# Another order for the opening of a feed-forward part: where the first block of M, the sums and the weight conversions are issued

## The chip, the core and the metric

The kernel runs on one core of a Trainium2 chip. The metric is the device time of one launch in microseconds (us). The profile names the engines as follows: PE is the matrix engine (PEld its weight load), DVE the vector engine, ACT the engine for activation functions, POOL the general engine, SP the engine that issues the loads. Each engine works through its own instructions in program order and waits at an instruction until what it reads is there and what it writes to is free.

## The reference

Three stages follow each other. Attention over 4 x 512 local tokens (a band of +-32 positions and 32 global tokens) and 4 x 32 global tokens gives x, 2176 rows of 512. A soft mixture of experts gathers x into 32 slots, runs an expert of two matrices on every slot, and hands the results back to the tokens by a second softmax. The last stage is a feed-forward part without a bias:

```python
    slot_out = slot_out.reshape(n_slots, D)
    c = np.exp(logits - logits.max(1, keepdims=True))
    c /= c.sum(1, keepdims=True) + 1e-09
    x = (c @ slot_out).astype(np.float32)
    h = x @ w_in
    g = h - np.tanh(h)
    return (g @ w_out).astype(np.float32)
```

All inputs and outputs are float32.

## The kernel before

The kernel never forms x of the last stage: h = c @ (slot_out @ w_in), and M = slot_out @ w_in has only 32 rows and 2048 columns. M and c are held in parts of rounded float32 (a high part and a remainder, 128 partitions in all), so that one rounded matmul of M against c gives h. g = h - tanh(h) is formed for small h as a polynomial, g_scaled = h (u - 2.5) u with u = h squared, and a flag computed at the end decides whether an exact second pass is needed.

The output is made of 17 tiles of 128 tokens. The feed-forward part runs in steps; a step is one chunk `fc` of 128 rows of w_out for a group of six (or five) tiles. One step: two heads (`g_head`, a matmul of 128x384 into one of two PSUM banks `h`, given out by `hbank()`), for each half of the tiles the square on ACT (`g_square`, line 1168), two operations on DVE (`g_tail0`, line 1174; `g_tail1`, line 1178, the last reader of the `h` bank), the rounded high part on ACT (`g_hi`, line 1185), the low part on POOL (`g_lo`, line 1189), and then per tile three matmuls (`ff`, lines 1202 to 1204): high x high, high x low, low x high of g and w_out, added up over the chunks in PSUM bank `a0` to `a5` of the tile. `gs_r` holds three sets of g, so heads run up to three steps ahead.

w_out comes as 64-bit words. `conv_head(c)` (ACT, line 535) and the four entries of `f32_tail` (an empty one, then DVE lines 539, 544, 549) turn chunk c into float32, `conv_ops(c)[4]` rounds it to `whi` (ACT, line 1062) and `[5]` makes `wlo` (POOL, line 1063). So `c1[1]`, `c1[2]`, `c1[3]` are DVE steps of chunk 1, `c1[4]` is ACT, `c1[5]` POOL.

The opening stands between the experts and the steps; it is written out by hand, line by line, and each engine gets its instructions in that order. The last expert matmuls (line 1036) leave the slot sums in `sop`, PSUM bank 5. They are scaled and copied to `sos` (line 1276), transposed and added up by four matmuls with `istk` (line 1279) and copied to `soT` (line 1280). Then M is made in blocks of 128, 384, 512, 512 and 512 columns: `m_rows(i, j)` (PE, line 1111, bank j), `m_rows_out(i)` (ACT, line 1120), `m_parts(i, j)` (PE, line 1125), `m_hi(i)` (ACT, line 1129) and `m_lo(i)` (DVE, line 1133). Blocks 0 to 2 fall in the opening; block 0 is all that the heads of step 0 need, block 1 serves the heads of steps 1 to 3. `keep_warm` (line 647) is a matmul whose result nobody reads. After the opening a loop over the steps follows; its first pass is step 1, `ff(1, ..)`.

Of the kernel before, what the change touches and what calls it, by code (L numbers as in the profile page):

```python
# [11 lines left out]
AF = mybir.ActivationFunctionType  # L12
ALU = mybir.AluOpType
# [49 lines left out]
def band_attention_soft_moe_tanhshrink_kernel(  # L63
# [15 lines left out]
    V, S, G, T, DMA = nc.vector, nc.scalar, nc.gpsimd, nc.tensor, nc.sync  # L79
# [454 lines left out]
    def f32_head(a, raw):  # L534
        S.activation(out=a.bitcast(F32), in_=raw[:, :, 1].bitcast(F32), func=AF.Abs, scale=2.0 ** -112)
# [110 lines left out]
    def keep_warm(bank, n):  # L646
        T.matmul(bank[:, 0:n], lhsT=ident, rhs=win[0][:, 0:n], skip_group_check=True)

    with tc.manual_schedule():
# [43 lines left out]
        for it in range(NG + 1):  # L693
# [33 lines left out]
            if gs is not None:  # L727
                c = global_probs(gs)
# [51 lines left out]
        f, rr = mrun[:, 10:11], mrun[:, 11:12]  # L780
# [31 lines left out]
        def diagonal(t, outer, n, step):  # L812
            return bass.AP(t.tensor, t.offset, [t.ap[0], (outer, n), (step + 4, 4), (1, 4)])
# [18 lines left out]
        whi, wlo, raw_o, val_t = {}, {}, {}, {}  # L832
# [66 lines left out]
        for g in range(2):  # L899
            V.tensor_copy(  # L900
                out=diagonal(siT[g][:, :, 16 * g:], 128, 4, 32),
                in_=sit[:, 0:128].rearrange("p (k g e s) -> p g k e s", k=4, g=2, e=4)[:, g],
# [12 lines left out]
        def bank(j):  # L915
            return psa.tile([128, 512], F32, tag=f"a{j}", name=f"a{j}")
# [4 lines left out]
        sop = bank(5)  # L921
# [126 lines left out]
        def conv_head(c):  # L1048
            if c < 16:
                f32_head(cv[0][:, c % 2], raw_o[c][0])  # L1050

        def conv_ops(c):
            if c >= 16:
                return [lambda: None] * 6
            raw, own = raw_o[c]
            r = slot(True)[0].rearrange("p (a f) -> p a f", a=2)
            whi[c], wlo[c] = r[:, 0, :].bitcast(F32R), r[:, 1, :].bitcast(F32R)
            w = cv[0][:, c % 2]
            wf = w.bitcast(F32)

            return f32_tail(w, raw, own) + [
                lambda: S.copy(out=whi[c], in_=wf),  # L1062
                lambda: G.tensor_tensor(out=wlo[c], in0=wf, in1=r[:, 0, :], op=ALU.subtract),  # L1063
            ]

        for u, (m, e) in enumerate(UNITS):
# [15 lines left out]
            k = CTURN.index(u) if u in CTURN else None  # L1082
            if k is not None:
                combine_turn(4 * k, 4 if k < 4 else 1)
            k = CPREP.index(u) if u in CPREP else None
# [21 lines left out]
        def m_rows(i, j):  # L1107
            lo, n = BLOCKS[i]
            pp = (hbank() if j is None else bank(j))[:, 0:n]
            for dc in range(4):  # L1110
                T.matmul(
                    pp[32 * dc:32 * dc + 32, :], lhsT=soT[:, dc, :], rhs=win[4 * (lo // 512) + dc][:, lo % 512:lo % 512 + n],
                    skip_group_check=True, tile_position=(0, 32 * dc),
                )
            mp_t[i] = pp

        def m_rows_out(i):
            n = BLOCKS[i][1]
            ms_t[i] = wk.tile([128, 512], F32, tag="sm", name="ms")[:, 0:n]
            S.copy(out=ms_t[i], in_=mp_t[i])  # L1120

        def m_parts(i, j):
            lo, n = BLOCKS[i]
            mp = (hbank() if j is None else bank(j))[:, 0:n]
            T.matmul(mp, lhsT=irep_m, rhs=ms_t[i])
            mp_t[i] = mp

        def m_hi(i):
            S.copy(out=mst(*BLOCKS[i]), in_=mp_t[i])

        def m_lo(i):
            lo, n = BLOCKS[i]
            V.tensor_tensor(
                out=mst(lo, n)[64:128], in0=mp_t[i][64:128, :], in1=mst(lo, n, F32)[64:128], op=ALU.subtract
            )
# [6 lines left out]
        gs_r = [[slot(True)[0][:, 0:768].bitcast(F32R) for _ in range(2)] for _ in range(3)]  # L1142
        n_u = 0
        steps = [(t0, nt, fc, fc == a, fc == b - 1) for t0, nt, a, b in PHASES for fc in range(a, b)]
        u_t, acc_t, part_t, room = {}, {}, {}, []
# [9 lines left out]
        def g_head(i, part):  # L1155
            nonlocal n_u
            t0, nt, fc = steps[i][:3]
            c = cols(i, part)
            n = c.stop - c.start
            h = hbank()[:, 0:n]  # L1160
            T.matmul(h, lhsT=mst(128 * fc, 128), rhs=cst(128 * t0 + c.start, n))  # L1161
            u, g = (r[:, n_u % 2, 0:n] for r in (u_r, g_r))
            n_u += 1
            u_t[i, part] = h, u, g

        def g_square(i, part):
            h, u, _ = u_t[i, part]
            S.activation(out=u, in_=h, func=AF.Square)  # L1168
# [3 lines left out]
        def g_tail0(i, part):  # L1172
            h, u, _ = u_t[i, part]
            V.scalar_tensor_tensor(out=h, in0=u, scalar=-2.5, in1=h, op0=ALU.add, op1=ALU.mult)  # L1174

        def g_tail1(i, part):
            h, u, g = u_t[i, part]
            V.tensor_tensor(out=g, in0=u, in1=h, op=ALU.mult)  # L1178
# [4 lines left out]
        def g_hi(i, part):  # L1183
            g, ghi, _ = g_parts(i, part)
            S.copy(out=ghi, in_=g)  # L1185

        def g_lo(i, part):
            g, ghi, glo = g_parts(i, part)
            G.tensor_tensor(out=glo, in0=g, in1=ghi.bitcast(F32), op=ALU.subtract)  # L1189
# [5 lines left out]
        def ff(i, tiles):  # L1195
            t0, nt, fc, first, last = steps[i]
            ghi, glo = gs_r[i % 3]
            for j in tiles:
                if first:
                    acc_t[j] = bank(tile_order(t0, nt).index(j))  # L1200
                c = slice(128 * j, 128 * j + 128)
                T.matmul(acc_t[j], lhsT=ghi[:, c], rhs=whi[fc], start=first, stop=False)  # L1202
                T.matmul(acc_t[j], lhsT=ghi[:, c], rhs=wlo[fc], start=False, stop=False)  # L1203
                T.matmul(acc_t[j], lhsT=glo[:, c], rhs=whi[fc], start=False, stop=last)  # L1204

        def keep_part(t0, j, scale):
            if not room:
                room.extend(two_rows())
            part_t[t0 + j] = room.pop(0)
            S.activation(out=part_t[t0 + j], in_=acc_t[j], func=AF.Copy, scale=scale)  # L1210
# [52 lines left out]
                V.tensor_reduce(out=am1, in_=amp, op=ALU.max, axis=AX.X)  # L1263
                V.tensor_scalar(out=flag, in0=am1, scalar1=THRESH, scalar2=None, op0=ALU.is_le)

        keep_warm(bank(0), 512)
        conv_head(0)
        c0 = conv_ops(0)
        c0[0]()
        c0[1]()  # L1270
        c0[2]()
        c0[3]()
        c0[4]()
        c0[5]()
        sos = wk.tile([128, 512], F32, tag="pt", name="sos")
        S.activation(out=sos, in_=sop, func=AF.Copy, scale=rr)
        sot = hbank()[:, 0:128]
        for dc in range(4):
            T.matmul(sot[:, 32 * dc:32 * dc + 32], lhsT=sos[:, 128 * dc:128 * dc + 128], rhs=istk, skip_group_check=True)
        V.tensor_copy(out=soT.rearrange("p k s -> p (k s)"), in_=sot)  # L1280
        conv_head(1)
        m_rows(0, 3)
        m_rows(1, 2)
        m_rows_out(0)
        c1 = conv_ops(1)
        c1[0]()
        m_rows(2, 3)
        c1[1]()
        m_parts(0, 0)
        c1[2]()  # L1290
        m_rows_out(1)
        m_parts(1, 2)
        c1[3]()
        m_hi(0)
        m_rows_out(2)
        m_lo(0)
        m_hi(1)
        g_head(0, 0)
        m_lo(1)
        c2 = conv_ops(2)  # L1300
        g_head(0, 1)
        g_square(0, 0)
        g_tail0(0, 0)
        g_tail1(0, 0)
        m_parts(2, 2)
        c1[4]()
        g_square(0, 1)
        g_head(1, 0)
        conv_head(2)
        g_tail0(0, 1)  # L1310
        c2[0]()
        keep_warm(bank(1), 256)
        g_hi(0, 0)
        g_square(1, 0)
        c1[5]()
        g_tail1(0, 1)
        g_tail0(1, 0)
        m_hi(2)
        g_hi(0, 1)
        g_head(1, 1)  # L1320
        c2[1]()
        g_lo(0, 0)
        ff(0, [0])
        g_lo(0, 1)
        ff(0, [1])
        g_square(1, 1)
        g_tail1(1, 0)
        g_tail0(1, 1)
        m_lo(2)
        g_hi(1, 0)  # L1330
        g_head(2, 0)
        g_square(2, 0)
        g_tail1(1, 1)
        g_lo(1, 0)
        ff(0, [4])
        g_tail0(2, 0)
        c2[2]()
        ff(0, [5])
        g_head(2, 1)
        g_hi(1, 1)  # L1340
        ff(0, [3])
        g_tail1(2, 0)
        ff(0, [2])
        g_square(2, 1)
        g_hi(2, 0)
        g_lo(1, 1)
        conv_head(3)
        g_tail0(2, 1)
        g_lo(2, 0)
        g_head(3, 0)  # L1350
        c2[3]()
        g_tail1(2, 1)
        g_square(3, 0)
        c2[4]()
        c2[5]()
        g_hi(2, 1)
        g_lo(2, 1)
        es_x.close()
# [1 line left out]
        for i, (t0, nt, fc, first, last) in enumerate(steps):  # L1360
# [4 lines left out]
            c = JOBS.get(i)  # L1365
# [3 lines left out]
            for part, tiles in enumerate((order[:half], order[half:])):  # L1369
# [43 lines left out]
                if part == 0:  # L1413
                    c = JOBS.get(i + 1)
# [32 lines left out]
    with tc.If(small < 1):  # L1447
        for t0, nt in [(0, 4), (4, 2), (6, 4), (10, 2), (12, 3), (15, 2)]:
            steps[:] = [(t0, nt, fc, fc == 0, fc == 15) for fc in range(16)]
            for i in range(18):  # L1450
                if i < 16:
# [3 lines left out]
                    u, g = (r[:, i % 2, 0:n] for r in (u_r, g_r))  # L1455
                    g_any(h, u, g, n)
                    ghi, glo = (x[:, 0:n] for x in gs_r[i % 3])
# [74 lines left out]
```

## Time and profile before

| | us |
|---|---|
| median of 3 runs | 403.67 (403.52 to 405.17) |
| profiled execution, its own time | 406.07 |
| its span, first to last instruction | 404.2 |
| PE busy | 380.3 (94%) |
| DVE busy | 275.7 (68%) |
| ACT busy | 218.2 (54%) |
| POOL busy | 208.3 (52%) |

The views show one profiled execution, with times from the start of its span. Ends of matmuls on PE are modelled. In a row with "xN" several instructions that follow each other on an engine are drawn together. "idle before" is the time for which the engine had nothing to do before the row, and the releaser is what ended it; a wait for several things is put down to the last one. An engine's share of the span is a mean over stages with different limits, so the stages are read one by one. The attention and the experts take the first 176 us, the opening lies between 175.8 and 184.7 us, and the steps of the feed-forward part fill the rest.

### The profile page before, as it was taken

The page shows a single profiled execution, that of the slowest core. Times are in us where ns is not written, and L with a number is a line of the kernel's source. Part 1 is how long each engine was busy: PE and PEld are TensorE (multiplying, and loading weights), DVE is VectorE, ACT ScalarE, POOL GpSimd, SP SyncE. Part 2 cuts the span into 40 slices and gives each one's busy share as a digit, 9 for nine tenths or more (in the row PEclk, how much of TensorE's full clock was granted, in tenths as well). Part 3 has the DMA queues.
Part 4 walks back from the last instruction along what each step waited for, and adds up shares of the span by engine and source line. Part 5 has one row for each costly group of instructions (what it writes and reads, how often), then busy time and mean ns, then how long its engine had stood idle before and what let it go on. Part 6 is the DMA issues. An engine that isn't in the chain of part 4 may idle for free.

```text
span 404.2 us, 10208 instructions
## 1 busy us (share of the span) xinstructions
PE 380.3 (94%) x3767; PEld 281.2 (70%) x3767; DVE 275.7 (68%) x832; ACT 218.2 (54%) x543; POOL 208.3 (52%) x275
## 2 busy tenths in 40 slices
PE   7979989989889899999999999999989999999994
PEld 3768778777677433336877786886868888888873
DVE  3577788776565546349998886697879997556541
ACT  2667877875566202248655645565575555445330
POOL 2567686666553010017866344455575667447441
PEclk9899999999999999999999999999999999999998
DMA  7799999999868899998203101003000003003004
GB/s 180 203 397 315 352 329 293 367 313 309 309 199 280 269 358 418 418 421 319 90 7 99 52 1 54 0 11 113 34 2 2 0 26 131 0 2 125 32 2 138
DMA packets 33978, 70.43 MB, mean 174 GB/s; under 512 B 3840, under 2 KB 10752, under 8 KB 33920
## 3 DMA queue, kind: packets, MB, share of 16 engines
q1 hardware_dynamic: 33776, 69.56, 50.8%
q8 instruction: 32, 0.52, 0.5%
q14 instruction: 26, 0.21, 0.2%
q10 hardware_dynamic: 144, 0.13, 0.1%
HBM read 65.22 MB, written 4.46 MB: 172 GB/s over the span
## 4 chain that ended last, share of the span: by engine, by line
PE 68%; DMA 9%; POOL 8%; issue 6%; DVE 5%; ACT 2%; SPq 0%; DVEq 0%; POOLq 0%; ACTq 0%
PE a L1204 13%; PE a L1203 13%; PE a L1202 13%; PE sc L248 8%; DMA slot<-in_w_dram 8%; PE X L281 4%; PE h L1161 4%; PE ptp L269 3%; POOL q L210 3%; PE gsc L434 3%; POOL slot L1189 2%; POOL v L210 2%; PE xgp L479 1%; DVE slot L1178 1%; POOL k L210 1%
## 5 line engine op out<-in xcount | busy, mean ns | idle before, releaser
L1189 POOL TENSOR_TENSOR slot<-slot 128x384 fp32r<-128x384 f32 x96 | 98.6, 1031 | 83.5 <-ACT slot L1185 81.6
L1202 PE MATMUL a<-slot 128*128 128x512 f32 x272 | 107.2, 394 | 1.3 <-ACT v_w L1210 0.7
L1204 PE MATMUL a<-slot 128*128 128x512 f32 x272 | 107.7, 396 | 0.0
L1203 PE MATMUL a<-slot 128*128 128x512 f32 x272 | 107.3, 394 | 0.0
L1174 DVE SCALAR_TENSOR_TENSOR h<-slot,h 128x384 f32<-128x384 f32 x96 | 51.5, 537 | 39.0 <-ACT slot L1168 38.7
L1185 ACT CAST slot<-slot 128x384 fp32r<-128x384 f32 x96 | 47.6, 496 | 49.0 <-DVE slot L1178 48.6
L1168 ACT ACTIVATE slot<-h 128x384 f32<-128x384 f32 x96 | 45.3, 473 | 34.9 <-PE h L1161 34.4
L1202 PEld LDWEIGHTS a<-slot 128*128 128x128 f32 x272 | 51.1, 188 | 13.8 <-ACT v_w L1210 1.4
L1204 PEld LDWEIGHTS a<-slot 128*128 128x128 f32 x272 | 51.0, 188 | 11.6
L1203 PEld LDWEIGHTS a<-slot 128*128 128x128 f32 x272 | 51.1, 188 | 9.2 <-POOL slot L1063 1.0
L1178 DVE TENSOR_TENSOR slot<-slot,h 128x384 f32<-128x384 f32 x96 | 50.9, 530 | 7.7 <-DVE h L1174 0.5
L258 ACT ACTIVATE sm<-sm,mb 128x128 f32<-128x128 f32 x128 | 41.2, 397 | 19.0 <-DVE mb L254 18.8
L248 PE MATMUL sc<-k,q 128*64 128x128 f32 x512 | 39.7, 297 | 4.8 <-POOL q L210 2.5
L248 PEld LDWEIGHTS sc<-k,q 128*64 128x64 f32 x512 | 33.8, 208 | 10.4 <-issue 5.1
L210 POOL TENSOR_SCALAR v<-v 32x1300 f32<-32x1300 f32 (+5 forms) x40 | 33.3, 833 | 12.7 <-PE xgp L479 8.6
L1063 POOL TENSOR_TENSOR slot<-k_w,slot 128x512 fp32r<-128x512 f32 x16 | 20.7, 1297 | 33.3 <-ACT slot L1062 33.3
L210 POOL TENSOR_SCALAR q<-q 64x256 f32<-64x256 f32 x62 | 28.1, 453 | 18.0 <-PE sc L248 7.9
L1161 PE MATMUL h<-slot 128*128 128x384 f32 x96 | 32.5, 341 | 0.8 <-DVE slot L1178 0.6
L254 DVE CUSTOM_DVE_ANT_0 sm<-sc,mask 128x128 f32<-128x128 f32 x128 | 30.1, 285 | 4.3 <-PE sc L248 3.8
L1161 PEld LDWEIGHTS h<-slot 128*128 128x128 f32 x96 | 17.9, 187 | 12.0 <-DVE slot L1178 5.9
L281 PE MATMUL X<-v,pt 128*32 128x65 f32 x1024 | 22.7, 223 | 2.4 <-issue 2.0
L281 PEld LDWEIGHTS X<-v,pt 128*32 128x32 f32 x1024 | 16.6, 109 | 7.3 <-issue 6.0
(244 smaller groups left out, 529.2 us busy)
## 6 DMA issues: line engine op xcount, KB each, us to landing
slot<-in_w_dram SPq DMA_DIRECT2D x54, 512.0 KB, 8.7
slot<-in_w_out_dram SPq DMA_DIRECT2D x9, 512.0 KB, 4.5
slot<-in_w_in_dram SPq DMA_DIRECT2D x16, 256.0 KB, 7.1
k<-in_k_dram SPq DMA_DIRECT2D x7, 576.0 KB, 8.0
q<-in_q_dram SPq DMA_DIRECT2D x15, 256.0 KB, 6.5
out_dram<-o SPq DMA_DIRECT2D x15, 256.0 KB, 2.4
slot<-in_w_in_dram SPq DMA_DIRECT2D x7, 512.0 KB, 9.8
v<-in_v_dram SPq DMA_DIRECT2D x8, 390.0 KB, 5.8
```

The lines of the kernel that those rows point to most:

```text
L210: G.tensor_scalar(out=o, in0=i, scalar1=0.0, scalar2=1.0, op0=ALU.add, op1=ALU.mult)
L248: T.matmul(sc[64 * i:64 * i + 64, a, :], lhsT=q_b[2][:, 256 * i + jj:256 * i + 256:4], rhs=k[:, i, :, WINDOWS[t][jj][0]], skip_group_check ...
L281: T.matmul(X[32 * jj:32 * jj + 32, h, :], lhsT=pt[:, 128 * jj + 32 * h:128 * jj + 32 * h + 32], rhs=v[:, WINDOWS[t][jj][0], 65 * h:65 * h ...
L1161: T.matmul(h, lhsT=mst(128 * fc, 128), rhs=cst(128 * t0 + c.start, n))
L1168: S.activation(out=u, in_=h, func=AF.Square)
L1174: V.scalar_tensor_tensor(out=h, in0=u, scalar=-2.5, in1=h, op0=ALU.add, op1=ALU.mult)
L1178: V.tensor_tensor(out=g, in0=u, in1=h, op=ALU.mult)
L1185: S.copy(out=ghi, in_=g)
L1189: G.tensor_tensor(out=glo, in0=g, in1=ghi.bitcast(F32), op=ALU.subtract)
L1202: T.matmul(acc_t[j], lhsT=ghi[:, c], rhs=whi[fc], start=first, stop=False)
L1203: T.matmul(acc_t[j], lhsT=ghi[:, c], rhs=wlo[fc], start=False, stop=False)
L1204: T.matmul(acc_t[j], lhsT=glo[:, c], rhs=whi[fc], start=False, stop=last)
```

## The change

The opening is issued in another order, and nothing is computed differently. The copy of the sums is cut into two halves of 256 columns, one on ACT and one on DVE. The warm-up matmul ahead of them has 256 columns in place of 512. Head and DVE steps of chunks 1 and 2 of w_out are issued earlier, partly ahead of the sums' copies. `m_rows` and `m_parts` use other banks, and `m_parts(0)` goes ahead of `m_rows(2)`. The first three tiles of step 0 are multiplied in two goes (`ff_first`): first the two terms with the high part of g, later the term with the low part; the remaining three tiles follow one by one between the heads of steps 1 and 2. Before, step 0 was multiplied tile by tile, in the order 0, 1, 4, 5, 3, 2, with both heads of step 1 ahead of it and the heads of step 2 between the tiles.

```diff
--- before.py
+++ after.py
@@ -1203,6 +1203,15 @@
                 T.matmul(acc_t[j], lhsT=ghi[:, c], rhs=wlo[fc], start=False, stop=False)
                 T.matmul(acc_t[j], lhsT=glo[:, c], rhs=whi[fc], start=False, stop=last)
 
+        def ff_first(terms, tiles):
+            ghi, glo = gs_r[0]
+            for j in tiles:
+                if terms.start == 0:
+                    acc_t[j] = bank(j)
+                c = slice(128 * j, 128 * j + 128)
+                for k, (g, w) in list(enumerate(((ghi, whi[0]), (ghi, wlo[0]), (glo, whi[0]))))[terms]:
+                    T.matmul(acc_t[j], lhsT=g[:, c], rhs=w, start=k == 0, stop=False)
+
         def keep_part(t0, j, scale):
             if not room:
                 room.extend(two_rows())
@@ -1263,96 +1272,90 @@
                 V.tensor_reduce(out=am1, in_=amp, op=ALU.max, axis=AX.X)
                 V.tensor_scalar(out=flag, in0=am1, scalar1=THRESH, scalar2=None, op0=ALU.is_le)
 
-        keep_warm(bank(0), 512)
         conv_head(0)
         c0 = conv_ops(0)
-        c0[0]()
-        c0[1]()
-        c0[2]()
-        c0[3]()
-        c0[4]()
-        c0[5]()
+        for f in c0:
+            f()
+        conv_head(1)
+        c1 = conv_ops(1)
+        c1[1]()
+        keep_warm(bank(0), 256)
         sos = wk.tile([128, 512], F32, tag="pt", name="sos")
-        S.activation(out=sos, in_=sop, func=AF.Copy, scale=rr)
+        S.activation(out=sos[:, 0:256], in_=sop[:, 0:256], func=AF.Copy, scale=rr)
+        V.tensor_scalar(out=sos[:, 256:512], in0=sop[:, 256:512], scalar1=rr, scalar2=None, op0=ALU.mult)
         sot = hbank()[:, 0:128]
         for dc in range(4):
             T.matmul(sot[:, 32 * dc:32 * dc + 32], lhsT=sos[:, 128 * dc:128 * dc + 128], rhs=istk, skip_group_check=True)
+        c1[2]()
+        conv_head(2)
         V.tensor_copy(out=soT.rearrange("p k s -> p (k s)"), in_=sot)
-        conv_head(1)
         m_rows(0, 3)
         m_rows(1, 2)
         m_rows_out(0)
-        c1 = conv_ops(1)
-        c1[0]()
-        m_rows(2, 3)
-        c1[1]()
-        m_parts(0, 0)
-        c1[2]()
+        c1[3]()
+        c2 = conv_ops(2)
+        c2[1]()
+        c1[4]()
+        c1[5]()
+        m_parts(0, 5)
+        m_rows(2, 1)
         m_rows_out(1)
-        m_parts(1, 2)
-        c1[3]()
+        c2[2]()
         m_hi(0)
+        m_lo(0)
+        g_head(0, 0)
+        g_head(0, 1)
         m_rows_out(2)
-        m_lo(0)
-        m_hi(1)
-        g_head(0, 0)
-        m_lo(1)
-        c2 = conv_ops(2)
-        g_head(0, 1)
+        m_parts(1, 4)
         g_square(0, 0)
+        c2[3]()
         g_tail0(0, 0)
         g_tail1(0, 0)
-        m_parts(2, 2)
-        c1[4]()
         g_square(0, 1)
+        m_parts(2, 5)
+        m_hi(1)
+        keep_warm(bank(0), 256)
+        g_hi(0, 0)
+        g_tail0(0, 1)
+        g_lo(0, 0)
+        g_tail1(0, 1)
+        m_hi(2)
+        ff_first(slice(0, 2), range(3))
+        g_hi(0, 1)
+        m_lo(1)
+        g_lo(0, 1)
         g_head(1, 0)
-        conv_head(2)
-        g_tail0(0, 1)
-        c2[0]()
-        keep_warm(bank(1), 256)
-        g_hi(0, 0)
         g_square(1, 0)
-        c1[5]()
-        g_tail1(0, 1)
+        ff_first(slice(2, 3), range(3))
+        m_lo(2)
+        c2[4]()
+        c2[5]()
         g_tail0(1, 0)
-        m_hi(2)
-        g_hi(0, 1)
+        ff(0, [3])
         g_head(1, 1)
-        c2[1]()
-        g_lo(0, 0)
-        ff(0, [0])
-        g_lo(0, 1)
-        ff(0, [1])
         g_square(1, 1)
         g_tail1(1, 0)
+        g_hi(1, 0)
+        g_lo(1, 0)
+        ff(0, [4])
         g_tail0(1, 1)
-        m_lo(2)
-        g_hi(1, 0)
         g_head(2, 0)
         g_square(2, 0)
         g_tail1(1, 1)
-        g_lo(1, 0)
-        ff(0, [4])
+        g_hi(1, 1)
+        g_lo(1, 1)
+        ff(0, [5])
         g_tail0(2, 0)
-        c2[2]()
-        ff(0, [5])
         g_head(2, 1)
-        g_hi(1, 1)
-        ff(0, [3])
+        g_square(2, 1)
         g_tail1(2, 0)
-        ff(0, [2])
-        g_square(2, 1)
         g_hi(2, 0)
-        g_lo(1, 1)
+        g_lo(2, 0)
         conv_head(3)
         g_tail0(2, 1)
-        g_lo(2, 0)
         g_head(3, 0)
-        c2[3]()
         g_tail1(2, 1)
         g_square(3, 0)
-        c2[4]()
-        c2[5]()
         g_hi(2, 1)
         g_lo(2, 1)
         es_x.close()
```

## Rows read from the trace of the kernel before

**Rows 1.** Stage table: busy time of each engine, granted clock, DMA share, GB/s.

```profile
core 0: us, PE busy (x) PEld busy (x) DVE busy (x) ACT busy (x) POOL busy (x), PEclk, DMA share, GB/s
175.80:184.70 8.90, 7.72 (x47) 3.55 (x47) 5.23 (x11) 6.22 (x14) 1.98 (x2) 1.00 1.03 420
189.50:396.50 207.00, 205.15 (x903) 162.76 (x902) 155.39 (x269) 112.52 (x245) 120.30 (x114) 1.00 0.12 41
```

**Rows 2.** Timeline of PE, 160 to 190: start, duration, instructions, [idle before, releaser].

```profile
176.69 0.97 PE L1279 MATMUL h<-istk,sos 128*128 128x32 f32 x8
178.05 1.93 PE L1111 MATMUL a<-win,mask 128*32 128x128 f32 x24 [0.38 <-DVE mask L1280]
179.92 1.14 PE L1125 MATMUL a<-ms,mask 128*128 128x128 f32 x4
181.09 0.62 PE L1161 MATMUL h<-slot 128*128 128x384 f32 x2
...
184.47 0.45 PE L1161 MATMUL h<-slot 128*128 128x384 f32 x1 [0.18 <-DVE slot L1178]
184.75 0.40 PE L1202 MATMUL a<-slot 128*128 128x512 f32 x1
...
189.53 0.40 PE L1202 MATMUL a<-slot 128*128 128x512 f32 x1
```

**Rows 3.** Timeline of ACT, 160 to 190, the steps of the chain.

```profile
175.85 0.69 ACT L1276 ACTIVATE sos<-a,mrun 128x512 f32<-128x512 f32 x1 [1.72 <-PE a L1036]
176.44 0.66 ACT L535 ACTIVATE k_w<-v_w 128x512 f32<-128x512 f32 x1
178.60 0.27 ACT L1120 COPY ms<-a 128x128 f32<-128x128 f32 x1 [1.51 <-PE a L1111]
179.25 0.48 ACT L1120 COPY ms<-a 128x384 f32<-128x384 f32 x1 [0.38 <-PE a L1111]
180.44 0.27 ACT L1129 CAST slot<-a 128x128 fp32r<-128x128 f32 x1 [0.72 <-PE a L1125]
...
183.41 0.52 ACT L1185 CAST slot<-slot 128x384 fp32r<-128x384 f32 x1
...
186.60 0.49 ACT L1168 ACTIVATE slot<-h 128x384 f32<-128x384 f32 x1 [0.22 <-PE h L1161]
```

**Rows 4.** Timeline of DVE, 160 to 190, the steps of the chain.

```profile
177.71 0.29 DVE L1280 COPY mask<-h 128x128 f32<-128x128 f32 x1 [4.23 <-PE h L1279]
177.91 0.42 DVE L539 TENSOR_SCALAR k_w<-k_w 128x512 int32<-128x512 int32 x1
178.37 0.69 DVE L544 SCALAR_TENSOR_TENSOR k_w<-v_w,k_w 128x512 int32<-128x512 int32 x1
...
180.74 0.29 DVE L1133 TENSOR_TENSOR slot<-a,slot 64x128 fp32r<-64x128 f32 x1 [0.96 <-ACT slot L1129]
...
182.21 0.56 DVE L1174 SCALAR_TENSOR_TENSOR h<-slot,h 128x384 f32<-128x384 f32 x1
182.80 0.55 DVE L1178 TENSOR_TENSOR slot<-slot,h 128x384 f32<-128x384 f32 x1
183.27 0.56 DVE L1174 SCALAR_TENSOR_TENSOR h<-slot,h 128x384 f32<-128x384 f32 x1
```

**Rows 5.** Timeline of SP: the issue of chunk 1 and a later issue.

```profile
166.04 0.33 SPq L104 DMA_DIRECT2D v_w<-in_w_out_dram  x1
...
176.07 0.33 SPq L104 DMA_DIRECT2D slot<-in_w_in_dram  x1
```

**Rows 6.** DMA issues, 165.5 to 166.5: count, size, us from issue to landing.

```profile
v_w<-in_w_out_dram SPq DMA_DIRECT2D x1, 512.0 KB, 10.0
```

**Rows 7.** Timeline of POOL, 160 to 190.

```profile
184.00 1.01 POOL L1189 TENSOR_TENSOR slot<-slot 128x384 fp32r<-128x384 f32 x1
```

**Rows 8.** Stage table of the start, columns as in the first group.

```profile
6.00:7.90 1.90, 0.01 (x1) 0.00 (x1) 0.85 (x9) 1.68 (x2) 0.00 (x0) 1.00 0.80 233
8.90:12.10 3.20, 3.20 (x27) 2.20 (x26) 1.72 (x11) 1.39 (x4) 1.30 (x4) 0.50 0.32 98
```

## The prediction

> **What bounds the kernel now.** I read the stage table first. From 189.5 us to 396.5 us TensorE is busy 205.15 of 207.00 us at a granted clock of 1.00 [rows 1]: in the feed-forward part PE is the bound, and nothing in that part changes. So whatever the opening gains or loses arrives at the end one for one, as the shift of one event: the first matmul of step 1, `ff(1, ..)`, at 189.53 [rows 2]. It is the first work after the edited stretch that both kernels issue in the same order. The opening, 175.80 to 184.70, is the other kind of stage: PE has 7.72 us of work in 8.90 us and no engine is full [rows 1], so there a chain of dependent steps sets the time. Read in order, it is: sum copy `sos` 175.85, its transposes 176.69, `soT` copied by 178.00, rows of M from 178.05, `m_parts` 179.92, first head 181.09, `g_hi(0,0)` 183.41, first `ff` 184.75 [rows 2 to 4]. From 184.75 to 189.53 PE issues the 18 matmuls of step 0 and three heads: 4.78 us, which 0.233 us a matmul and 0.2 us a head account for.
>
> **Part 1, the sums.** Before, ACT copies all 512 columns in 0.69 us and the transposes follow 0.15 us after its end [rows 2, 3]. After, ACT takes 256 columns and DVE 256. No row has that size; the ends are 0.27 (128 columns, ACT) or 0.29 (DVE) and 0.69 us (512) [rows 3, 4], I take 0.42 for both, near the middle as the column count is. Alone this would save about 0.3 us. But two other steps are moved ahead of it. `conv_head(1)` now stands before the ACT half, `c1[1]` before the DVE half. Both engines work in program order, and `conv_head(1)` reads chunk 1 of w_out, whose load SP issued at 166.04 [rows 5]. Loads of that stretch land 10.0 us after issue [rows 6], and SP's eighth issue after it comes at 176.07 [rows 5], which is 10.0 us on as well: the queue moves at the pace of the landings. So the data are there at about 176.05, after the last matmul that the sums need (the old copy could start at 175.85). Before, `conv_head(1)` came at 176.44, behind the copy [rows 3], and hid the load completely. Now the added wait holds the sums behind it:
> - ACT: `conv_head(1)` 176.07 to 176.73 (0.66), its half 0.10 us before that ends (as at 176.44 against 176.54 [rows 3]), 176.63 to 177.05.
> - DVE: `c1[1]` 176.78 (0.42), the DVE half 0.46 us later (177.91 to 178.37 [rows 4]), 177.24 to 177.66.
> - PE: the second half of the transposes starts 0.15 us later at 177.81 and takes half of 0.97 [rows 2]: 178.30. `c1[2]`, now ahead of the `soT` copy on DVE, takes 0.69 [rows 4] and ends at 178.35, so it is hidden, just. `soT` 178.35 to 178.64, against 178.00: **0.64 us later**.
>
> `conv_head(2)`, also moved up, reads a load issued one place later, there at about 177.3; ACT is free from 177.05 until the first `m_rows_out`, so it costs nothing. No DMA is issued in the moved steps, and SP's order is the same.
>
> The Trainium skill, DMA: Bandwidth & Descriptors, section Anatomy of one DMA, fits the time of a DMA as about 2.0 us plus its bytes over 436 GB/s; for 512 KB this is an estimate of 3.2 us, so chunk 1 would be there by 169.3 and the moved head would be free. It is a fit for another issuing path; the 10.0 us of the trace speaks against it here, and by it the time would be that of the first rival below.
>
> **Part 2, from `soT` to the first head.** Before: 178.00 to 181.09, 3.09 us. `m_rows(2, 3)` stood in front of `m_parts(0)` on PE, and had to wait for bank 3; so `m_parts(0)` began at 179.92 although its input was copied by 178.87 [rows 2, 3]. After, `m_parts(0, 5)` is in front. Then ACT is next: `m_rows_out(0)` 0.55 us after the rows start (178.05 to 178.60), at 179.24 to 179.51; `c1[4]` (512 columns on ACT, like the 0.66 row) must wait for `c1[3]` on DVE (178.56 to 179.25) and runs 179.5 to 180.1; then `m_rows_out(1)` (0.48) and `m_hi(0)` (0.27), to 180.77; `m_lo(0)` 0.03 later for 0.29; the head 0.06 later [rows 3, 4], 181.1. DVE's `c2[1]` and `c2[2]` (0.42 + 0.69) fit between 179.25 and 180.8. **Gain 0.64 us, which puts the first head where it was** (181.1 against 181.09).
>
> **Part 3, to the first `ff`.** From the head: its square 0.48 us later for 0.49, 0.03, then the two tails 0.59 apart with 0.55 for the second [rows 3, 4], `g_hi(0,0)` 0.06 later for 0.52, PE 0.1 later: 183.9. `c2[3]` lies between `m_lo(0)` and the square's end. Before, `g_hi(0,0)` was over by 183.93, but the first `ff` stood behind head (1,1), which waited for a tail until 184.47 [rows 2, 3]. `ff_first` with terms 0 and 1 on three tiles needs no low part, so POOL (first low part 184.00, 1.01 us [rows 7]) is not asked for. The shorter warm-up and `m_parts(1)`, `m_parts(2)` fill PE from 181.5 to about 183.6 and end before. **First `ff` 0.85 us earlier.**
>
> **Part 4, from the first `ff` to step 1.** The same 18 matmuls, but five heads instead of three: 18 x 0.233 + 5 x 0.2 = 5.19 us if PE never waits. It waits. Before, four tiles (2.8 us of PE) lay between head (2,0) and head (3,0); after, one. A head needs one of two `h` banks, and that is free when the second tail of the head two places ahead is done. Count from the first `ff` at F: head (1,0) F+1.4, low terms 0.7, tile 3 0.7, head (1,1) at F+3.0. Its result is there 0.45 later, square 0.49, tail 0.03 later, second tail 0.59 on; the next pair 0.47 on, its second tail again 0.59 on for 0.55, then 0.06 [rows 2 to 4]: head (3,0) at F+3.0+3.23. `ff(1, ..)` is at F+6.43 = **190.33**, with 1.24 us of idle PE at heads (2,1) and (3,0). POOL has four operations of about 1.01 us [rows 7] from F to the low part that step 1 reads first, and 6.4 us for them.
>
> **Sum.** Sums +0.64, rows of M and head -0.64, head to first `ff` -0.85 (with the removed place behind head (1,1)), step 0 4.78 to 6.43, +1.65: **+0.8 us**. The profiled execution has a span of 404.2 and took 406.07; the three runs have a median of 403.67. The sum is a difference, so I put it on the median: **404.5 us**.
>
> **Rivals.**
> - The load costs nothing (it is there earlier, or the halves really run together): ACT's half at 175.85, `soT` over at about 177.74, 0.90 us earlier than in my sum: 403.6. For it: the gap is only 0.2 us between 175.85 and 176.07. Against: both rows of SP; for the head to run in ACT's idle time before 175.85, the load would have to land some 0.9 us before SP's issue says.
> - PE is not starved in part 4 (squares and tails closer than the pitch above): 5.19 instead of 6.43, 403.3. For it: DVE has shed `c2`'s three operations there. Against: the chain is of dependent steps, which a freer DVE doesn't shorten. With the first rival together: 402.4.
> - Slower: TensorE's clock. The first warm-up matmul is halved and PE has gaps of 0.6 to 0.8 us around 176.4 and 178.5. At the start of the run PE was busy 0.01 us in 6.0 to 7.9, and then the granted clock was 0.50 (1.2 GHz) from 8.9 to 12.1 [rows 8]. If the same 3.2 us at half rate fell on step 0, they would cost 1.6 us more: 406.1. It decides from the point where the gaps join into one as long as that one was; the transposes and rows of M lie between them, which speaks against.
>
> **How the numbers follow.** Mine 0.60 (404.5), load free 0.15 (403.6), PE fed 0.12 (403.3), both 0.05 (402.4), clock 0.08 (406.1). The range takes in the first three with the spread of the runs shown (403.52 to 405.17) and the unknown size of the 256-column copies (0.15 us either way): 402.7 to 405.9. Half a per cent, about what a measurement of this kernel can tell from no change, is 2.0 us: 401.65 to 405.69. Only the clock case and a disturbed run lie above, and only a miss larger than both favourable cases lies below: faster 0.05, same 0.86, slower 0.09.
>
> **What would show it.** Right: `conv_head(1)` on ACT starting near 176.1 with a wait for a DMA, and the ACT half behind it at about 176.6; the first head within 0.3 us of 181.1; first `ff` near 183.9; PE idle before heads (2,1) and (3,0), about 1.2 us together; `ff(1, ..)` near 190.3. Wrong: a first sum copy at 175.85, PE without gaps from the first `ff` on, or a granted clock below 1.00 between 176 and 190.

## The result, and the profile after

The changed kernel takes 406.72 us (median of 18 runs) against 403.91 us before (18 runs). The ratio leaves out the three slowest of its executions, which lie over 1.5% above its fastest: 1.0059, 95% interval 1.0033 to 1.0084, that is +2.4 us. 404.5 us with a range of 402.7 to 405.9 us was forecast. The sign of the small shift was right, its size was not: a loss beyond half a per cent had been given 9 in 100.

The profiled execution has a span of 406.4 us, 2.2 us more than before. Since the attention and the experts end at slightly different times in each execution, I measure the opening from the start of its first warm-up matmul to the first matmul of step 1, and call that **the stretch**. Before it is 175.73 to 189.53, 13.80 us. After it is 174.92 to 191.56, 16.64 us: 2.84 us more. The stage tables of before and of after, both cut at the end of the `soT` copy, the first head and the first `ff`, show where:

```profile
core 0: us, PE busy (x) PEld busy (x) DVE busy (x) ACT busy (x) POOL busy (x), PEclk, DMA share, GB/s
175.73:178.00 2.27, 1.94 (x12) 1.26 (x10) 0.29 (x2) 1.24 (x2) 0.00 (x0) 1.00 1.04 426
178.00:181.09 3.09, 3.00 (x28) 1.05 (x29) 2.01 (x4) 1.39 (x4) 0.00 (x0) 1.00 1.01 415
181.09:184.75 3.66, 2.90 (x8) 1.35 (x9) 2.98 (x6) 3.63 (x9) 2.02 (x2) 1.00 1.03 422
184.75:189.53 4.78, 4.78 (x22) 3.77 (x22) 4.72 (x10) 3.32 (x8) 3.57 (x4) 1.00 0.91 369
```

```profile
174.92:177.85 2.93, 1.85 (x12) 1.33 (x10) 1.74 (x5) 1.70 (x3) 0.68 (x1) 1.00 1.03 419
177.85:181.87 4.02, 3.96 (x27) 1.30 (x27) 2.57 (x6) 1.53 (x4) 1.27 (x1) 0.58 1.03 422
181.87:184.83 2.96, 2.55 (x13) 1.41 (x9) 1.73 (x5) 2.30 (x6) 0.00 (x0) 1.00 1.03 421
184.83:191.56 6.73, 5.71 (x24) 4.30 (x25) 5.23 (x10) 4.62 (x10) 5.18 (x5) 1.00 0.89 365
```

The second stage of after is the surprise. Its granted clock (the third number from the right) is 0.58 on the mean; looked at closer, it is 0.50 (1.2 GHz) from 177.9 to 181.3. There PE is busy 3.96 of 4.02 us: at half its clock it has become the limit of a stage that took 3.09 us before. The timeline of PE shows what it did ahead of the fall:

```profile
174.92 0.70 PE L647 MATMUL a<-win,ident 128*128 128x256 f32 x2
176.37 1.15 PE L1288 MATMUL h<-istk,sos 128*128 128x32 f32 x8 [0.75 <-ACT sos L1284]
177.91 1.93 PE L1111 MATMUL a<-win,mask 128*32 128x128 f32 x16 [0.38 <-DVE mask L1291]
...
181.87 0.62 PE L1161 MATMUL h<-slot 128*128 128x384 f32 x2
...
184.83 1.67 PE L1213 MATMUL a<-slot 128*128 128x512 f32 x6 [0.41 <-ACT slot L1185]
...
190.14 0.44 PE L1161 MATMUL h<-slot 128*128 128x384 f32 x1 [0.33 <-DVE slot L1178]
191.28 0.44 PE L1161 MATMUL h<-slot 128*128 128x384 f32 x1 [0.69 <-DVE slot L1178]
191.56 0.40 PE L1202 MATMUL a<-slot 128*128 128x512 f32 x1
```

A warm-up of 0.70 us, 0.75 us idle, eight matmuls of only 32 columns, 0.38 us idle, and then the rows of M begin and the clock is at one half. In the kernel before the warm-up reached up to the transposes without a gap ([rows 2], 176.69 without a wait). Later PE waits 0.33 and 0.69 us at heads (2,1) and (3,0); before, PE was busy for all of the 4.78 us from the first `ff` to step 1.

ACT and DVE show the added wait itself:

```profile
175.29 0.66 ACT L535 ACTIVATE k_w<-v_w 128x512 f32<-128x512 f32 x1 [1.05 <-DMA v_w<-in_w_out_dram]
175.85 0.46 ACT L1284 ACTIVATE sos<-a,mrun 128x256 f32<-128x256 f32 x1
```

```profile
175.98 0.43 DVE L539 TENSOR_SCALAR k_w<-k_w 128x512 int32<-128x512 int32 x1 [2.39 <-ACT k_w L535]
176.35 0.48 DVE L1285 TENSOR_SCALAR sos<-a,mrun 128x256 f32<-128x256 f32 x1
...
177.56 0.29 DVE L1291 COPY mask<-h 128x128 f32<-128x128 f32 x1
```

`conv_head(1)` waited 1.05 us for its load (the v_w DMA) and held the ACT half of the sums until 175.85, 0.93 us after the warm-up began; before, the copy began 0.12 us after it ([rows 2, 3] and the start of the stretch, 175.73). The DVE half stands behind `c1[1]` and begins 0.50 us after the other half.

So the theory after the comparison, **theory A**: the reordering costs time by itself, and beside that the wait at the sums leaves PE idle, whereupon its clock falls to one half for a while. **Rival B**: the fall is chance (both traces have others, in the attention), and all of the loss lies in the order.

### The profile page after: what moved, and what is told of

Its sections match the earlier page's. It is cut to its first block, busy times and chain, and to the rows that moved or that the text cites. A ratio compares the mean times of both kernels' runs of the same rounds, so it can differ in the third digit from the quotient of the medians.

```text
span 406.4 us, 10212 instructions
## 1 busy us (share of the span) xinstructions
PE 382.0 (94%) x3767; PEld 282.1 (69%) x3767; DVE 276.2 (68%) x833; ACT 219.0 (54%) x543; POOL 207.6 (51%) x275
## 4 chain that ended last, share of the span: by engine, by line
PE 76%; DMA 6%; issue 5%; DVE 4%; POOL 4%; ACT 3%; SPq 1%; DVEq 0%; ACTq 0%
PE a L1203 14%; PE a L1204 14%; PE a L1202 14%; PE sc L248 8%; PE h L1161 4%; PE X L281 4%; PE ptp L269 3%; PE a L997 3%; DMA slot<-in_w_dram 3%; DMA v_w<-in_w_out_dram 2%; PE gsc L434 2%; POOL q L210 2%; PE xTp L317 1%; PE xgp L479 1%; DVE slot L1178 1%
## 5 line engine op out<-in xcount | busy, mean ns | idle before, releaser
L1189 POOL TENSOR_TENSOR slot<-slot 128x384 fp32r<-128x384 f32 x96 | 97.2, 1016 | 89.5 <-ACT slot L1185 87.1
L1202 PE MATMUL a<-slot 128*128 128x512 f32 x269 | 106.0, 394 | 1.3 <-ACT v_w L1219 0.7
L1204 PE MATMUL a<-slot 128*128 128x512 f32 x269 | 106.6, 396 | 0.0
L1203 PE MATMUL a<-slot 128*128 128x512 f32 x269 | 106.2, 395 | 0.0
L1202 PEld LDWEIGHTS a<-slot 128*128 128x128 f32 x269 | 50.5, 188 | 13.9 <-ACT v_w L1219 1.4
L1204 PEld LDWEIGHTS a<-slot 128*128 128x128 f32 x269 | 50.5, 188 | 11.4
L1203 PEld LDWEIGHTS a<-slot 128*128 128x128 f32 x269 | 50.5, 188 | 9.2 <-POOL slot L1063 1.1
```

## Experiments

All numbers of the stretch are us from its start, from one profile each. "Clock" is the granted clock between `soT` and the first head; "mean clock" that of whole executions, averaged over them. Times are set against the kernel before, measured beside it; the 86 executions of before are those measured beside the experiments.

| kernel | `soT` | first head | first `ff` | step 1 | clock | ratio (95%) | mean clock (executions) |
|---|---|---|---|---|---|---|---|
| before | 2.27 | 5.36 | 9.02 | 13.80 | 1.00 | | 0.9952 (86) |
| after | 2.93 | 6.95 | 9.91 | 16.64 | 0.58 | 1.0059 (1.0033 to 1.0084) | 0.9931 (18) |
| e5, after again | 3.00 | 5.47 | 8.42 | 15.15 | 1.00 | 1.0048 (1.0022 to 1.0075) | 0.9914 (12) |
| e1, after + warm-up | 3.01 | 5.49 | 8.44 | 15.17 | 1.00 | 1.0007 (0.9978 to 1.0035) | 0.9959 (12) |
| e2, sums first | 2.13 | 4.60 | 7.80 | 14.49 | 1.00 | 1.0011 (0.9977 to 1.0045) | 0.9948 (12) |
| e3, before + wait | 3.08 | 6.17 | 9.83 | 14.61 | 1.00 | 1.0000 (0.9966 to 1.0035) | 0.9956 (12) |
| e4, before, warm-up halved | 2.26 | 5.35 | 9.02 | 13.79 | 1.00 | 0.9979 (0.9952 to 1.0007) | 0.9952 (12) |
| e6, heads early | 2.90 | 6.75 | 10.03 | 16.52 | falls | 1.0058 (1.0032 to 1.0083) | 0.9908 (12) |
| e7, both repairs | 2.14 | 4.62 | 7.90 | 13.55 | 1.00 | 0.9981 (0.9954 to 1.0008) | 0.9958 (12) |
| e8, after, no warm-up | 2.83 | 6.63 | 9.58 | 16.31 | falls | 1.0076 (1.0047 to 1.0105) | 0.9913 (11) |
| e9, e6 with squares early | 3.01 | 6.83 | 10.11 | 16.21 | falls | one execution | |
| e10, e7 with `c1[5]` early | 2.14 | 4.61 | 7.90 | 13.32 | 1.00 | 1.0010 (0.9980 to 1.0040) | 0.9942 (12) |

For e8, which has no first warm-up, the stretch is counted from the end of the last expert matmuls. Single executions of one kernel differ by several us (402.62 to 410.36 for the changed kernel), and the stretch itself begins anywhere between 172.9 and 175.7 us in these profiles; so a ratio resolves about 0.3% (1.2 us), while the stretch of kernels with the same steps repeats closely (13.80 and 13.79, 15.15 and 15.17).

### e1: the wait stays, PE is kept at work

```diff
+        keep_warm(bank(0), 512)
         keep_warm(bank(0), 256)
         sos = wk.tile([128, 512], F32, tag="pt", name="sos")
```

> The changed kernel with one more warm-up matmul of 512 columns ahead of the sums, so that PE has work while the halves of the sums wait. Stretch looked at: from the first warm-up matmul to the first matmul of step 1, 13.8 us before and 16.6 us in the changed kernel's profile. Theory A (the added wait leaves PE idle, the granted clock falls to 0.50 for some 3.4 us, and this makes the forecast +0.8 us into +2.4): clock 1.00 through the opening, stretch 14.6 to 14.9 us, ratio to the kernel before about 1.002. Rival B (the fall is chance, as others in both traces, and the order of step 0 is what costs): stretch 16.0 to 16.6, ratio about 1.006 as the changed kernel.

The stage between `soT` and the first head, and PE ahead of it:

```profile
176.67:179.15 2.48, 2.42 (x27) 0.83 (x27) 2.17 (x6) 1.33 (x4) 1.06 (x1) 1.00 1.03 420
```

```profile
173.66 1.88 PE L647 MATMUL a<-win,ident 128*128 128x512 f32 x4
175.37 0.97 PE L1289 MATMUL h<-istk,sos 128*128 128x32 f32 x8
176.73 1.07 PE L1111 MATMUL a<-win,mask 128*32 128x128 f32 x16 [0.38 <-DVE mask L1292]
```

The transposes follow the warm-up without a gap, the clock stays at 1.00, the stage takes 2.48 in place of 4.02 us, and over 12 executions the mean clock is that of the kernel before. With one more matmul that nobody reads, the stretch is 1.47 us shorter than in the profile of after. One profile can't show that the matmul did it (e5 below has 15.15 us without it); the ratio, whose interval ends at 1.0035 and so leaves out B's 1.006, and the mean clock speak for A. But the stretch is 15.17, above A's 14.6 to 14.9: in the stretch **the order alone costs 1.37 us**, not the 0.8 forecast. The whole time shows less, 1.0007 or +0.3 us; its interval reaches up to +1.4 us and just takes in the 1.37.

### e2: the sums first, no wait ahead of them

```diff
-        conv_head(1)
-        c1 = conv_ops(1)
-        c1[1]()
         keep_warm(bank(0), 256)
...
         V.tensor_scalar(out=sos[:, 256:512], in0=sop[:, 256:512], scalar1=rr, scalar2=None, op0=ALU.mult)
+        conv_head(1)
+        c1 = conv_ops(1)
+        c1[1]()
...
-        c1[2]()
         conv_head(2)
         V.tensor_copy(out=soT.rearrange("p k s -> p (k s)"), in_=sot)
+        c1[2]()
```

(`c1[4]`, `c1[5]`, `c2[2]` and `c2[3]` move back by a few lines as the expectation says, and so does `m_rows_out(2)`, which it doesn't name.)

> The changed kernel with the conversion steps taken out of the sums' way: head of chunk 1 and its first DVE step behind the two halves, its second behind the copy of soT, its rounding behind the first high part of M, and the last two steps of chunk 2 behind the first low part and the first tails. No wait for a load is left ahead of the sums. Theory A: gap of PE before the transposes at most 0.3 us, clock 1.00, soT some 0.9 us earlier than in the changed kernel, stretch 13.5 to 13.9 us, ratio to before 0.999 to 1.000. Rival B: only the 0.9 us come back, stretch about 15.7, ratio about 1.004.

```profile
173.55 0.47 ACT L1281 ACTIVATE sos<-a,mrun 128x256 f32<-128x256 f32 x1 [0.70 <-PE a L1036]
173.92 0.66 ACT L535 ACTIVATE k_w<-v_w 128x512 f32<-128x512 f32 x1
```

The half of the sums starts 0.12 us into the stretch and the head of chunk 1 behind it finds its load there. `soT` is 0.87 us earlier than in e5, as expected, and the clock holds. Yet the stretch is 14.49, in between A (13.5 to 13.9) and B (15.7): from the first `ff` to step 1 it is 6.69 us as in after (6.73), so the loss inside step 0 is there with a full clock and without the wait. The stretch fits neither theory as stated. The ratio, 1.0011 (0.9977 to 1.0045), takes in both.

### e3 and e4: the wait alone, the small warm-up alone

```diff
+        conv_head(1)
         sos = wk.tile([128, 512], F32, tag="pt", name="sos")
...
-        conv_head(1)
         m_rows(0, 3)
```

> The kernel before with one line moved: the head of chunk 1 goes ahead of the copy of the sums (which stays whole, on ACT). The wait for the load alone, without the rest of the change. Theory A: the copy starts about 0.8 us later, PE gets a gap of some 0.5 us behind the warm-up of 512 columns; stretch 14.6 us where the clock holds and 16 to 16.4 us where it falls, ratio 1.002 to 1.006. Rival B: clock 1.00, stretch 14.6 us, ratio 1.002.

```profile
173.29 0.69 ACT L535 ACTIVATE k_w<-v_w 128x512 f32<-128x512 f32 x1 [0.54 <-DMA v_w<-in_w_out_dram]
173.87 0.68 ACT L1277 ACTIVATE sos<-a,mrun 128x512 f32<-128x512 f32 x1
```

```profile
172.93 1.12 PE L647 MATMUL a<-win,ident 128*128 128x512 f32 x2
174.60 1.08 PE L1280 MATMUL h<-istk,sos 128*128 128x32 f32 x8 [0.54 <-ACT sos L1277]
176.06 1.50 PE L1111 MATMUL a<-win,mask 128*32 128x128 f32 x20 [0.38 <-DVE mask L1281]
```

The moved head waits for the same DMA, the copy starts 0.94 us into the stretch in place of 0.12, and step 1 comes 0.81 us later, 14.61: the price of the wait by itself, as forecast. The clock holds, with 0.54 us idle behind a warm-up of 512 columns. Both theories allowed for this, so e3 doesn't tell them apart; in the ratio, 1.0000 (0.9966 to 1.0035), the 0.81 us can't be seen.

```diff
-        keep_warm(bank(0), 512)
+        keep_warm(bank(0), 256)
```

> The kernel before with the first warm-up matmul cut from 512 to 256 columns and nothing else. PE gets a gap of 0.3 to 0.5 us while the sums are copied. Theory A, if so small a gap is enough: the clock falls in part of the executions, ratio 1.001 to 1.004. Theory A with the longer wait needed, and rival B: clock 1.00, stretch 13.8 us or a little less, ratio 1.000.

13.79 us against 13.80, mean clock as before. Half the warm-up without the wait costs nothing.

### e5 and e8: how often the clock falls

> The changed kernel once more, unaltered, beside the others on one chip: a second profile of the opening, and more executions with their mean granted clocks. With the clock at 1.00 the run with one more warm-up took 15.17 us from the first warm-up matmul to step 1, against 13.80 before: the order alone costs 1.4 us. Theory A (the rest of the 2.4 us is the clock, which falls in the opening in a part of the executions): stretch 15.1 us where the clock holds or 16.6 us where it falls, mean clock of the executions 0.001 to 0.002 under that of the kernel before, ratio 1.004 to 1.006. Rival B (the rest was scatter of the executions): stretch 15.1 us, clock as before, ratio 1.003.

e5 is the changed kernel unaltered. Its profile is one in which the clock held in the opening (it fell twice in the attention):

```profile
177.06:179.53 2.47, 2.41 (x26) 0.83 (x26) 2.15 (x6) 1.33 (x4) 1.06 (x1) 1.00 1.03 420
...
182.48:189.21 6.73, 5.70 (x23) 4.29 (x24) 5.24 (x10) 4.61 (x10) 5.18 (x5) 1.00 1.02 417
```

2.47 us in place of 4.02 for the same instructions, and a stretch of 15.15 in place of 16.64: **a fall in the opening costs 1.5 us**. The mean clock of these 12 executions, 0.9914, is 0.004 under before, more than A's 0.001 to 0.002; B had it as before. With the 18 of the first measurement it is 0.9924, against 0.9952 of 86 executions of before (standard errors 0.0006 and 0.0003). The ratio, 1.0048 (1.0022 to 1.0075), leaves B's 1.003 possible; the mean clock doesn't.

```diff
-        keep_warm(bank(0), 256)
         sos = wk.tile([128, 512], F32, tag="pt", name="sos")
```

> The changed kernel without its first warm-up matmul, so that PE has nothing at all to do while the sums wait (1.4 to 1.5 us). Theory A: the granted clock falls in more of the executions than in the changed kernel, mean clock of the executions 0.001 or more under the changed kernel's, stretch (taken from the end of the last expert matmuls) 16.6 us in the profile, ratio 1.006 to 1.008. Rival B: clock as in the kernel before, stretch 15.1 us, ratio 1.003.

```profile
174.25 1.15 PE L1287 MATMUL h<-istk,sos 128*128 128x32 f32 x8 [1.35 <-ACT sos L1283]
```

```profile
176.60:180.00 3.40, 3.40 (x15) 1.17 (x12) 1.75 (x4) 1.48 (x4) 1.38 (x1) 0.50 1.02 419
```

With 1.35 us idle ahead of the transposes the clock is 0.50 in 176.6 to 180.0, and the ratio is 1.0076, both as A said; the stretch is 16.31, 0.3 us short of A's. The mean clock, 0.9913, is under before's as in the changed kernel. That it is 0.001 under the changed kernel's isn't shown: e5, measured beside it, has 0.9914.

Taken together, warm-up against wait: without the wait the clock holds with 512 (before) and 256 columns (e4, e2, e7, e10); with the wait it holds with 512 (e3) and 768 (e1) and falls with 256 (after, e6, e9, not in e5's profile) and none (e8). In the profiles, 4 of 5 kernels or repeats with the wait and a short warm-up or none show the fall, and none of 7 others. The mean clocks go the same way: 0.9918 over the 53 executions of after, e5, e6 and e8, against 0.9953 over the 72 of e1 to e4, e7 and e10 (standard error 0.0004 each).

### e6 and e9: heads earlier in step 0

Of the lines that e6 and e7 move, the edits below show the new places of the main ones.

```diff
         g_hi(0, 0)
+        m_lo(1)
+        g_head(1, 0)
         g_tail0(0, 1)
...
+        g_head(1, 1)
         ff_first(slice(2, 3), range(3))
...
+        g_head(2, 0)
+        ff(0, [3])
...
+        ff(0, [4])
...
         g_head(2, 1)
+        ff(0, [5])
```

> The changed kernel with the heads of steps 1 and 2 issued earlier, as far ahead of the work that hides them as in the kernel before: the low part of block 1 ahead of the second pair of tails, head (1,0) before ff_first, head (1,1) before its second go, head (2,0) before tile 3, head (2,1) before tile 5. Tests the idle PE of step 0: from the first ff to step 1 it was 6.73 us, with 5.2 us of work in it. If the heads' chain is what PE waits for there: 5.2 to 5.6 us, and the stretch 1.1 to 1.4 us shorter than the changed kernel's at the same clock (13.7 to 14.1 with clock 1.00). If ACT and DVE are full there and the order of the heads makes no difference: 6.5 to 6.8 us.

```profile
183.30 0.44 PE L1161 MATMUL h<-slot 128*128 128x384 f32 x1 [0.29 <-DVE slot L1133]
183.58 1.55 PE L1213 MATMUL a<-slot 128*128 128x512 f32 x6
```

From the first `ff` to step 1: 6.49 us, a miss on the first branch and just under the second. Even the 0.24 us less than in after is hardly a gain: head (1,0) now stands ahead of the first `ff`, 0.28 us, and so outside what is counted. From the first head of step 0 to step 1 it is 9.77 us (by the table), against 9.69 in after. The clock fell in this profile as well, before the first `ff`, but it still covered the first two heads, which took 0.78 us in place of 0.62. ACT and DVE show why the early heads won so little:

```profile
184.46 0.52 ACT L1185 CAST slot<-slot 128x384 fp32r<-128x384 f32 x1 [0.78 <-DVE slot L1178]
184.88 0.48 ACT L1168 ACTIVATE slot<-h 128x384 f32<-128x384 f32 x1
```

```profile
185.40 0.56 DVE L1174 SCALAR_TENSOR_TENSOR h<-slot,h 128x384 f32<-128x384 f32 x1 [0.97 <-ACT slot L1168]
```

DVE stood idle for 0.97 us, because I had left square (1,0) behind `g_hi(0,1)` on ACT, which waited for a tail: the head was early and its square wasn't. e9 puts that right (against e6):

```diff
+        g_square(1, 0)
         g_hi(0, 1)
         g_lo(0, 1)
-        g_square(1, 0)
         g_head(1, 1)
```

(and `g_square(1, 1)` ahead of `c2[4]`)

> The sixth experiment with its squares put right: there square (1,0) stood on ACT behind g_hi(0,1), which waited for a tail, so DVE idled 0.97 us and the earlier head won nothing (first ff to step 1 6.49 us). Now square (1,0) goes ahead of g_hi(0,1), and square (1,1) ahead of the rounding of chunk 2. If the chain head, square, tails is what PE waits for: first ff to step 1 5.5 to 5.8 us as in the seventh experiment (5.65), against 6.73 in the changed kernel. If something else holds it: 6.3 to 6.5 us again.

10.11 to 16.21: 6.10 us, between the two branches (5.5 to 5.8 and 6.3 to 6.5), and the wait has moved on:

```profile
188.31 0.56 DVE L1178 TENSOR_TENSOR slot<-slot,h 128x384 f32<-128x384 f32 x1 [0.78 <-POOL slot L1189]
```

```profile
186.01 1.29 POOL L1063 TENSOR_TENSOR slot<-k_w,slot 128x512 fp32r<-128x512 f32 x1 [0.42 <-ACT slot L1062]
187.26 1.97 POOL L1189 TENSOR_TENSOR slot<-slot 128x384 fp32r<-128x384 f32 x2
```

The second tail of head (2,0) writes the `g` buffer of head (1,0), which POOL must have read for its low part; that stands behind `c2[5]`, 1.29 us, which the change moved forward. A head's way is thus bound by two buffers, `h` and `g`. So the first branch is right in kind and wrong in its size: heads alone won at most 0.1 us, heads with their squares 0.3 to 0.5 us (9.38 from the first head to step 1, against 9.69 in after, with the first two heads at half clock again), and POOL's queue is next.

### e7 and e10: both repairs together

The order of e2 up to `m_hi(0)`, then heads as in e9, `c2[3]` to `c2[5]` late as in the kernel before, no second warm-up:

```diff
+        m_lo(1)
+        m_parts(2, 5)
+        g_hi(0, 0)
+        g_head(1, 0)
...
+        g_square(1, 0)
+        ff_first(slice(0, 2), range(3))
+        g_hi(0, 1)
+        g_lo(0, 1)
+        g_head(1, 1)
+        c1[5]()
```

> Both repairs together, as a version that may beat both kernels: sums first as in the second experiment, heads early as in the sixth, the last step of chunk 2 late as in the kernel before, and no second warm-up. Expected from the parts: soT 2.13 us after the first warm-up, first head at 4.6, first ff at 7.5, 5.2 us from there: stretch 12.6 to 13.0 us against 13.80 before, ratio 0.997 to 0.998. If the low parts on POOL hold step 0 up instead: 13.5 to 14 us, ratio 1.000.

```profile
185.70 0.56 DVE L1178 TENSOR_TENSOR slot<-slot,h 128x384 f32<-128x384 f32 x1 [0.33 <-POOL slot L1189]
```

13.55 us, 0.25 us under before; from the first `ff` 5.65 us. Up to the first head all is as expected, the first `ff` is 0.4 us late, and DVE waits 0.33 us for POOL. The 12.6 to 13.0 us hoped for is missed; the stretch is that of the second branch, in which POOL holds step 0 up. e10 moves one line:

```diff
         c1[4]()
+        c1[5]()
         g_tail0(0, 1)
...
         g_head(1, 1)
-        c1[5]()
```

> The seventh experiment with the low part of chunk 1's weights one place earlier on POOL, ahead of the second low part of step 0. There the second tail of head (2,0) waited 0.33 us for POOL to finish reading the g buffer that it writes. Expected: that wait gone, head (3,0) about 0.3 us earlier, stretch 13.2 to 13.4 us (13.55 there, 13.80 before), ratio 0.997 to 0.998. If POOL only shifts the wait to the low parts of step 0: 13.5 to 13.7 us.

```profile
173.30:186.62 13.32, 12.05 (x70) 7.33 (x66) 10.81 (x21) 9.52 (x21) 6.33 (x6) 1.00 1.03 420
```

13.32 us, 0.48 us under before, with no wait for POOL left there and the clock at 1.00. In time neither can be told from before: 1.0010 (0.9980 to 1.0040) for e10, which had been expected at 0.997 to 0.998, and 0.9981 (0.9954 to 1.0008) for e7. So in these profiles the opening is shorter than before, by 0.1% of the kernel, which the times don't resolve.

## Why the prediction was wrong, point by point

- **That a shift of step 1 arrives at the end one for one: right for these two profiles.** From there to the end of the profile it is 214.67 us before and 214.84 after (214.4 to 216.0 in the other profiles).
- **The sums (part 1): right.** +0.64 us at `soT` was forecast; e5 measures 3.00 against 2.27, +0.73, and after +0.66. `conv_head(1)` waited for its DMA, and e3 gives the wait alone as 0.81 us. By the fit in the Trainium skill's DMA: Bandwidth & Descriptors, section Anatomy of one DMA, the load would have been there long before the sums (an estimate of 3.2 us for 512 KB). The trace of after disagrees: there this load took 10.0 us, and the head waited 1.05 us for it; as the prediction says, the page gives its fit for another issuing path. The first rival (load free) falls with it.
- **`soT` to first head (part 2): right at full clock.** 2.46 us forecast, 2.47 in e5. In after it is 4.02, which is the clock.
- **To the first `ff` (part 3): 0.15 us short.** 2.80 forecast, 2.95 in e5.
- **Step 0 (part 4): right in kind, 0.3 us short.** PE waits at heads (2,1) and (3,0), 0.33 and 0.69 us by the rows of after. 6.43 us forecast, 6.73 measured in after, e1 and e5 alike: from a tail to the second tail of the same head it was mostly 0.66 or 0.67 us, not 0.59 (the rows below), and a head that PE had to wait for takes 0.28 us to the next matmul, not 0.2. The second rival (PE fed) falls. That POOL has time enough for its four operations, `c2[5]` among them, held only because the chain was slower still; e9 shows POOL as the next limit.

```profile
188.87 0.56 DVE L1174 SCALAR_TENSOR_TENSOR h<-slot,h 128x384 f32<-128x384 f32 x1 [0.35 <-ACT slot L1168]
189.53 0.55 DVE L1178 TENSOR_TENSOR slot<-slot,h 128x384 f32<-128x384 f32 x1
190.00 0.56 DVE L1174 SCALAR_TENSOR_TENSOR h<-slot,h 128x384 f32<-128x384 f32 x1
190.67 0.56 DVE L1178 TENSOR_TENSOR slot<-slot,h 128x384 f32<-128x384 f32 x1
```

- **The sum at full clock** was thus +0.8 forecast and +1.35 measured (15.15 against 13.80): 0.1 us missed at the sums, 0.15 to the first `ff`, 0.3 in step 0. On the 403.67 us that I started from this is 405.0, still inside the range.
- **The clock: the step that failed.** The sum put it at nothing. It stood as the third rival, at 406.1 us, with 8 chances in 100, with the right cause (gaps of PE) and about the right price (1.6 us forecast, 1.5 measured), though placed on step 0, where the profiles show it on the rows of M. A granted clock below 1.00 between 176 and 190 was one of my signs of being wrong, and it came. The step that put it there was "it decides from the point where the gaps join into one as long as that one was", 1.9 us of nothing, with the transposes and rows of M between them as evidence against. The runs show that this was the wrong point: in after the clock fell behind gaps of 0.75 and 0.38 us with eight matmuls of 32 columns between them, and in 4 of the 5 profiles with the wait and a short warm-up or none. I had named the halved warm-up and the gaps, but looked for one long gap. Each of the two alone is small (e4, e3); together they are not.
- **The two add up.** If each fall of 3.4 us at half clock takes 1.7 of 404 us from the mean clock (0.0042), the difference between 0.9952 and 0.9924 is 0.67 falls an execution more than before. That estimate times 1.5 us is 1.0 us; with 1.35 us for the order it makes 2.35 us, against 2.4 measured (1.3 to 3.4 by the interval). So close an agreement is luck: the whole time of e1 puts the order at +0.3 us, with up to +1.4 in its interval, and would leave more to the clock. That it is the opening where the falls lie is shown by profiles (4 of 5 against 0 of 7), not execution by execution.

So both the order and the clock have a part in the loss. By the stretches the order's is the larger; how the 2.4 us divide between them, the whole times don't settle.

## What to carry to other kernels

When a step that reads from a DMA is moved ahead of work that the matrix engine waits for, look up when that load lands, to a tenth of a us; the old place may have hidden it by an accident of the order. Where a change at once shortens filler work on the matrix engine and lengthens the wait that the filler covered, price the two together and give the clock a real chance. And work that keeps PE fed is a stock: spending it earlier (three tiles at once) only helps if the chain that refills it is moved forward too, through every buffer that it passes.

## What the runs showed of the hardware

That the granted clock can fall behind gaps of only 0.75 and 0.38 us was not expected; the other fall in the trace of after followed one long gap:

```profile
92.45 0.26 PE L281 MATMUL X<-v,pt 128*32 128x65 f32 x2 [2.00 <-issue]
```

```profile
92.30:95.80 3.50, 3.35 (x53) 2.25 (x54) 1.14 (x4) 0.00 (x0) 1.05 (x1) 0.54 1.07 296
```

PE was idle 2.00 us, without anything that the profile shows as a cause, and the clock was 0.54 on the mean of the next 3.5 us. The Trainium skill, TensorE: Matmul & The Clock Gate, section Part 1, says that the clock follows how busy the engine has been of late; the runs agree in that both ways of being less busy, one long gap or short gaps around matmuls of few columns, were followed by 0.50. Which gaps are enough is not settled: e5's profile kept 1.00 with 0.38, 0.33 and 0.38 us around its transposes, and e9's fell with nearly the same:

```profile
175.14 0.63 PE L1288 MATMUL h<-istk,sos 128*128 128x32 f32 x4 [0.38 <-ACT sos L1284]
176.10 0.63 PE L1288 MATMUL h<-istk,sos 128*128 128x32 f32 x4 [0.33 <-DVE sos L1285]
177.12 1.07 PE L1111 MATMUL a<-win,mask 128*32 128x128 f32 x16 [0.38 <-DVE mask L1291]
```

```profile
174.11 0.63 PE L1288 MATMUL h<-istk,sos 128*128 128x32 f32 x4 [0.42 <-ACT sos L1284]
175.04 0.63 PE L1288 MATMUL h<-istk,sos 128*128 128x32 f32 x4 [0.30 <-DVE sos L1285]
176.06 1.24 PE L1111 MATMUL a<-win,mask 128*32 128x128 f32 x16 [0.38 <-DVE mask L1291]
```

So such gaps came with a fall in 4 of 5 profiles, and don't decide it in a single execution.

The copies of 256 columns from PSUM took 0.46 us on ACT and 0.48 on DVE, where I had put 0.42 between the rows for 128 and 512 columns.
